# Moving 160 columns of the last down-projection chunk into an earlier load, and folding with two full-width products

## The chip, the core and the metric

The kernel runs on one core of a Trainium2 chip. Its time is the device time of one execution in microseconds (us). The median of three runs of the kernel before is 263.67 us (263.55 to 263.82).

## The reference

One decoding step of a transformer block for 8 sequences, in float32. Attention with 32 query heads over 4 key/value heads looks at the last 1024 cached positions; a gated feed-forward layer of width 3584 follows.

```python
h  = x + softmax(q(LN(x)) @ K.T * 128**-0.5) @ V @ wo      # K, V: last 1024 of 4096 positions
g  = LN(h) @ w_gate                                        # (8, 3584)
u  = LN(h) @ w_up
h2 = h + (gelu(g) * u) @ w_down                            # w_down: (3584, 1024)
```

The 111 MB of weights and caches are read once; the arithmetic on 8 rows is small.

## The kernel before

All weights and caches stream through two SBUF buffers, `wbuf[0]` and `wbuf[1]`, of 64 KB per partition each. One queue, SyncE's (SP), issues every load in program order: twelve units of 8 MB that alternate between the buffers, then the parts of `w_down`. `w_down` has 28 chunks of 128 rows. The first eight ride in other units. Sixteen go into `wbuf[0]` as `wd0` (12 chunks) and `wd1` (4). The last four go into `wbuf[1]`: `we0` holds two chunks (`last - 3` and `last - 2`), `we1` one (`last - 1`), and the last chunk, numbered `last`, is split by columns into `wl0` (160 of every 256 columns) and `wl1` (the other 96).

TensorE (PE) works with tiles of 128 x 32: four column groups of the array run side by side, each on its own 32 output partitions. Each product in float32 appears in the trace as two MATMUL records. In the tail, output partitions `32j .. 32j+31` hold columns `256j .. 256j+255` of the result, so that one chunk is four products of 256 columns (`QW`), one per column group.

A loop on PE (`half`, line 227 in the profile) makes the big products. Its last pass, `half_a(6)`, multiplies `wd0` and `wd1` and leaves the sums in the bank pair `sums[0]`. VectorE (DVE) adds these to the residual in the tile `d1` (lines 430 and 431). Behind the loop stands straight code on PE, in this order: chunks `last - 3` and `last - 2` into the bank `acc` (they wait for `we0`); the fold, four products of `add2` with `d1`, which bring `d1` into the layout by column groups; chunk `last - 1` (waits for `we1`); then the last chunk's 160 columns into the bank `fin` (wait for `wl0`) and its 96 columns into `sums[1]` (wait for `wl1`). ScalarE (ACT) copies the whole of `acc` to the tile `most` (line 450). DVE adds `most` and each bank into `o_fin` (line 464), and two stores of `o_fin` end the program: `out0` (160 columns) from SP's queue and `out1` (96 columns) from ACT's. Line 96 is the helper that issues every DMA. Three memsets on DVE, `ahead` (line 455), wait for `we1` ahead of the final adds. GpSimd (POOL) prepares constants at the start.

Of the kernel before, what the change touches and what calls it, by code (L numbers as in the profile page):

```python
# [7 lines left out]
P = 128  # L8
B = 8
D = 1024  # L10
# [5 lines left out]
NQ = 4  # L16
QW = D // NQ
N = 512
# [11 lines left out]
PARTS = (12, 4)  # L30
ENDPARTS = (2, 1)
ENDS = (160, 96)
# [12 lines left out]
class Flow:  # L45
# [37 lines left out]
    def run(self, engine, make, *waits, mark=True, gives=None):  # L83
        ins = self.start(engine, make, waits)
        if gives is not None:
            ins.then_inc(*gives)
            return None
        if not mark:
            return None
        self.done[engine] += 1  # L90
        ins.then_inc(self.own[engine], 1)
        return self.own[engine], self.done[engine]

    def move(self, name, out, src, *waits, engine="sync", sem=None):
        s = self.sem(name) if sem is None else sem
        self.start(engine, lambda e: e.dma_start(out, src), waits).then_inc(s, 16)  # L96
        return s, 16


def decode_block(nc, x, units, dn, tails, ends, outs):  # L100

    fl = Flow(nc)
    run, move = fl.run, fl.move
# [3 lines left out]
    def sb(name, *shape):  # L107
        return nc.alloc_sbuf_tensor(name, list(shape), F32).ap()

    def bank(name, n):  # L110
        return nc.alloc_psum_tensor(name, [P, n], F32).ap()

    space = sb("w", P, 2 * BUF)
    wbuf = [space[:, i * BUF:(i + 1) * BUF] for i in range(2)]
    sums = [bank(f"sum{i}", 2 * N) for i in range(2)]
    turned = bank("turned", 2 * N)
    acc, fin = bank("acc", N), bank("fin", N)
# [25 lines left out]
    def half_a(k, h=1):  # L143
        return at_mark["a", k, h]

    def half_b(k, h=1):
        return at_mark["b", k, h]
# [5 lines left out]
    for u in range(UNITS):  # L153
        k, i = divmod(u, 2)
# [7 lines left out]
    for i, (n, sem) in enumerate(zip(PARTS, (go[0], *go_later[1:]))):  # L162
        c0 = (q0 - EARLY) * D
# [2 lines left out]
    assert q0 == EARLY + HEAD  # L166
    arrived = {}
    c0 = 0
    for i, n in enumerate(ENDPARTS):
        here = move(f"we{i}", wbuf[1][:, c0:c0 + n * D], tails[i], half_b(nb - 1))  # L170
        for r in range(n):
            arrived[q0] = wbuf[1][:, c0 + r * D:c0 + (r + 1) * D], here
            q0 += 1
        c0 += n * D
    last = q0
    assert last == DF // P - 1
    blocks = []
    a = 0
    for i, (n, src) in enumerate(zip(ENDS, ends)):
        t = wbuf[1][:, c0:c0 + NQ * n]  # L180
        blocks.append((a, n, t, move(f"wl{i}", t, src)))
        c0 += NQ * n
        a += n


    ident = sb("ident", P, P)
    z = run("gpsimd", lambda e: e.memset(ident, 0.0))
# [8 lines left out]
    add2 = sb("add2", P, 2, 32)  # L196
    run("gpsimd", lambda e: e.tensor_add(
        add2.rearrange("p c m -> p (c m)"), ident[:, 0:2 * 32], ident[:, 2 * 32:4 * 32]), id_ok)
    note = sb("note", 1, 8)
    for i, g in enumerate(go_later):  # L200
        run("gpsimd", lambda e: e.memset(note[:, i:i + 1], 0.0), gives=(g, GATE[i] * (passes - 1)))

    own = sb("own", P, HB)
# [30 lines left out]
    with PE.Fori(1, TURNS) as i:  # L234
        with PE.If(i != NO_B[0]):
            with PE.If(i != NO_B[1]):
                half(1, [(0, (go[1], 17))])
                take(go_fold, 1)
                for ch in range(2):
                    ins = PE.matmul(turned[0:32, ch * N:(ch + 1) * N], add2[:, ch, :], y_sb,  # L240
                                    start=True, stop=True)
# [52 lines left out]
    for hf in range(2):  # L294
        done = (half_a, half_b)[hf]
        q_sb = sb(f"q{hf}", P, N)
        tok = run("vector", lambda e: e.tensor_scalar(  # L297
            q_sb, sums[hf][:, 0:N], scale, None, op0=ALU.mult), done(0, 0))
# [23 lines left out]
    for hf in range(2):  # L322
        done = (half_a, half_b)[hf]
        nmax, tot, rtot = (sb(f"{n}{hf}", P, 1) for n in ("nmax", "tot", "rtot"))
        share.append(sb(f"share{hf}", P, HB))
        tok = run("vector", lambda e: e.tensor_reduce(  # L326
            out=nmax, in_=sums[hf], axis=AX.X, op=ALU.max, negate=True), done(1))
# [5 lines left out]
        tok = run("vector", lambda e: e.reciprocal(rtot, tot), p_ok)  # L333
# [6 lines left out]
    for hf in range(2):  # L340
        done = (half_a, half_b)[hf]
        o_sb = sb(f"o{hf}", P, DH)
        tok = None
        for h in range(2):
            o3 = sums[hf][:, h * N:(h + 1) * N].rearrange("p (b d) -> p b d", b=HB)
            for b in range(HB):
                end = h == 1 and b == HB - 1
                out = source[:, hf * DH:(hf + 1) * DH] if end else o_sb
                if h == 0 and b == 0:
                    tok = run("vector", lambda e: e.tensor_scalar(  # L350
                        out, o3[:, b], share[hf][:, b:b + 1], None, op0=ALU.mult), done(2, h))
                else:
                    tok = run("vector", lambda e: e.scalar_tensor_tensor(  # L353
                        out, o3[:, b], share[hf][:, b:b + 1], o_sb, op0=ALU.mult, op1=ALU.add),
                        tok, done(2, h), mark=not end,
                        gives=(go_turn, 1) if end and hf else None)
# [11 lines left out]
    tok = run("scalar", lambda e: e.copy(y_sb, sums[0][:, 0:N]), half_a(3, 0))  # L368
    tok = run("vector", lambda e: e.tensor_add(y_sb, y_sb, sums[0][:, N:2 * N]), tok, half_a(3))  # L369
    tok = run("vector", lambda e: e.tensor_add(y_sb, y_sb, sums[1][:, 0:N]), tok, half_b(3, 0))  # L370
# [13 lines left out]
    at = sb("at", P, DF // P, 32)  # L384
# [3 lines left out]
    for k, n in enumerate(SETS):  # L388
        rows = 32 * n
        tok = run("scalar", lambda e: e.copy(gate[:rows], sums[0][:rows, 0:N]), half_a(4 + k, 0))  # L390
        tok = run("vector", lambda e: e.tensor_add(  # L391
            gate[:rows], gate[:rows], sums[0][:rows, N:2 * N]), tok, half_a(4 + k))
        ge_ok = run("scalar", lambda e: e.activation(ge[:rows], gate[:rows], AF.Gelu_apprx_tanh), tok)
        if k == 1:
# [5 lines left out]
        tok = run("scalar", lambda e: e.copy(up[:rows], sums[1][:rows, 0:N]), half_b(4 + k, 0))  # L400
        tok = run("vector", lambda e: e.tensor_add(  # L401
            up[:rows], up[:rows], sums[1][:rows, N:2 * N]), tok, half_b(4 + k))
        run("vector", lambda e: e.tensor_mul(source[:rows, 0:N], up[:rows], ge[:rows]), tok, ge_ok,
            gives=(go_turn, 1))
        t = turned[:, 0:N].rearrange("p (i m) -> p i m", m=P)
        at_ok = run("vector", lambda e: e.tensor_copy(
            at[:, q0:q0 + 4 * n, :].rearrange("p (j i) m -> p i j m", j=n),
            t[:, :, 0:rows].rearrange("p i (j m) -> p i j m", j=n)), at_mark["t", 6 + k])
# [6 lines left out]
        else:  # L415
# [3 lines left out]
                at_ok, gives=(go_later[0], 1))  # L419
# [3 lines left out]
    tok = run("vector", lambda e: e.tensor_add(  # L423
        down[rows:P], down[rows:P], sums[1][rows:P]), half_b(5), side_ok)
    for ch in range(2):
        p0 = 32 * (2 + ch)
        tok = run("vector", lambda e: e.tensor_copy(
            rest[p0:p0 + 32], down[rows:P, ch * N:(ch + 1) * N]), tok)
    d1 = sb("d1", P, N)
    tok = run("vector", lambda e: e.tensor_add(d1, rest, sums[0][:, 0:N]), tok, half_a(6, 0))  # L430
    d1_ok = run("vector", lambda e: e.tensor_add(d1, d1, sums[0][:, N:2 * N]), tok, half_a(6))


    def quarters(lhs, rhs, *waits, start=False, stop=False):
        for j in range(NQ):
            tok = run("tensor", lambda e: e.matmul(
                acc[32 * j:32 * j + 32, 0:QW], lhs(j), rhs(j), start=start, stop=stop),
                *waits, mark=(stop and j == NQ - 1))
        return tok

    def chunk(q, **flags):
        t, here = arrived[q]
        return quarters(lambda j: at[:, q, :], lambda j: t[:, j * QW:(j + 1) * QW], here, at_ok, **flags)

    chunk(last - 3, start=True)
    chunk(last - 2)
    quarters(lambda j: add2[:, j // 2, :], lambda j: d1[:, (j % 2) * QW:(j % 2) * QW + QW], d1_ok)
    tok = chunk(last - 1, stop=True)
    most = sb("most", P, QW)
    most_ok = run("scalar", lambda e: e.copy(most, acc[:, 0:QW]), tok)  # L450


    ahead = sb("ahead", 1, AHEAD)
    for i in range(AHEAD):
        run("vector", lambda e: e.memset(ahead[:, i:i + 1], 0.0), arrived[last - 1][1], d1_ok)

    o_fin = sb("o_fin", P, QW)
    done = []
    for (c0, n, t, here), d_ps in zip(blocks, (fin, sums[1])):
        for j in range(NQ):  # L460
            tok = run("tensor", lambda e: e.matmul(  # L461
                d_ps[32 * j:32 * j + 32, 0:n], at[:, last, :], t[:, j * n:(j + 1) * n],
                start=True, stop=True), here, d1_ok, mark=(j == NQ - 1))
        done.append(run("vector", lambda e: e.tensor_add(  # L464
            o_fin[:, c0:c0 + n], most[:, c0:c0 + n], d_ps[:, 0:n]), most_ok, tok))

    for e in both:
        nc.engines[e].br_ne(lap, 0, on_true="never", on_false="through")
    with nc.body("never", valid_engines=both):
        nc.regs_alu(lap, lap, 1, op=ALU.add)  # L470
        for e in both:
            nc.engines[e].br_lt(lap, 9, on_true="never", on_false="through").branch_hint(near[e])
    nc.switch_bb("through")

    cut = ENDS[0]
    sent = [move("out0", outs[0], o_fin[:, 0:cut], done[0]),
            move("out1", outs[1], o_fin[:, cut:QW], done[1], engine="scalar")]


    issued = fl.sem("issued")  # L480
# [86 lines left out]
```

## Time and profile before

| | |
|---|---|
| median of the runs | 263.67 us |
| profiled execution, its own time | 263.59 us |
| span of its profile | 262.3 us |
| TensorE busy, share of the span | 54% |
| VectorE busy | 17% |
| ScalarE busy | 5% |
| data moved, mean rate | 111.31 MB, 424 GB/s |

The profile's span runs from the first to the last instruction; the execution's time is 1.3 us longer. In a timeline the columns are the start in us from the span's beginning, the duration in us, the engine, the line, the operation with what it writes and reads, and in brackets the idle time ahead of it with what ended it. "PEld" is a load of weights into TensorE's array, which overlaps PE. The end of a MATMUL record is modelled, so its start is the safer number.

### The profile page before, as it was taken

To read this page: it belongs to the slowest core of one execution; us is meant where nothing else is said; L and a number is where in the kernel's file an instruction comes from. 1 tells how busy PE (TensorE), PEld (TensorE's weight loads), DVE (VectorE), ACT (ScalarE), POOL (GpSimd) and SP (SyncE) were. 2 spreads that over 40 slices of the span, in tenths; PEclk is the share of its full clock that TensorE was granted. 3 is DMA by queue.
4 is the path that set the end of the run, shared out by engine and by line. 5 is a ranking of instruction groups with operands and counts; after the bars stand their busy time and mean duration, and the time that the engine had idled before them with its cause. 6 is when DMAs were issued, how large, how long until landed. Compare 5 with 4: busy or idle time off the path is not lost. (4 is left out here: it accounts for less than half of the span.)

```text
span 262.3 us, 2262 instructions
## 1 busy us (share of the span) xinstructions
PE 141.3 (54%) x972; PEld 45.1 (17%) x972; DVE 43.8 (17%) x115; ACT 13.5 (5%) x19; POOL 7.7 (3%) x18
## 2 busy tenths in 40 slices
PE   0025805926606927707908508827709809409986
PEld 0021201212101312102302102122102202103232
DVE  0340200240100140400410100264100300100522
ACT  1000000000120010000000200000300000200000
POOL 5000100100000000100100000000000000000000
PEclk9999985986965995956966965975956956858999
DMA  8997997999799799979979998997999999799895
GB/s 320 485 470 330 480 480 340 460 480 460 340 480 480 320 480 480 460 340 480 480 320 480 480 420 380 480 480 320 480 480 400 400 480 480 320 440 480 370 424 226
DMA packets 2896, 111.31 MB, mean 424 GB/s; under 512 B 456, under 2 KB 712, under 8 KB 976
## 3 DMA queue, kind: packets, MB, share of 16 engines
q1 hardware_dynamic: 2736, 111.23, 98.4%
q10 hardware_dynamic: 160, 0.08, 0.1%
HBM read 111.18 MB, written 0.13 MB: 424 GB/s over the span
## 5 line engine op out<-in xcount | busy, mean ns | idle before, releaser
L227 PE MATMUL sum<-w,still 128*32 128x512 f32 x832 | 116.3, 721 | 96.8 <-PEq L214 96.8
L227 PEld LDWEIGHTS sum<-w,still 128*32 128x32 f32 x832 | 32.5, 130 | 176.8 <-issue 176.7
L245 PE MATMUL turned<-ident,source 128*128 128x128 f32 x64 | 10.4, 315 | 20.9 <-PEq L214 20.9
L245 PEld LDWEIGHTS turned<-ident,source 128*128 128x128 f32 x64 | 8.3, 161 | 26.2 <-issue 26.2
L240 PE MATMUL turned<-y_sb,add 128*32 128x512 f32 x24 | 11.3, 592 | 0.9 <-PEq L214 0.9
L326 DVE TENSOR_REDUCE nmax<-sum 128x1 f32<-128x1024 f32 x2 | 2.4, 1224 | 28.4 <-PE sum L227 28.4
L401 DVE TENSOR_TENSOR up<-up,sum 128x512 f32<-128x512 f32 (+1 forms) x2 | 1.4, 684 | 32.2 <-PE sum L227 32.2
L297 DVE TENSOR_SCALAR q<-sum 128x512 f32<-128x512 f32 x2 | 1.4, 692 | 25.7 <-PE sum L227 25.7
L282 DVE COPY still<-turned 128x1024 f32<-128x1024 f32 x4 | 4.7, 1219 | 4.2 <-PE turned L245 4.2
L391 DVE TENSOR_TENSOR gate<-gate,sum 128x512 f32<-128x512 f32 (+1 forms) x2 | 1.4, 686 | 23.8 <-PE sum L227 23.8
L353 DVE SCALAR_TENSOR_TENSOR o<-sum,share,o 128x128 f32<-128x128 f32 x12 | 4.2, 350 | 4.2 <-PE sum L227 3.8
L350 DVE TENSOR_SCALAR o<-sum,share 128x128 f32<-128x128 f32 x2 | 0.7, 350 | 22.9 <-PE sum L227 22.9
L328 ACT ACT_TABLE_LOAD x1 | 1.3, 1283 | 59.0 <-DVE nmax L326 59.0
L357 POOL MEMSET still<- 128x1024 f32 x2 | 1.9, 952 | 74.3 <-PE sum L227 74.3
L240 PEld LDWEIGHTS turned<-y_sb,add 128*32 128x32 f32 x24 | 2.6, 110 | 8.7 <-issue 8.7
L369 DVE TENSOR_TENSOR y_sb<-y_sb,sum 128x512 f32<-128x512 f32 x1 | 0.7, 689 | 16.0 <-PE sum L227 16.0
L370 DVE TENSOR_TENSOR y_sb<-y_sb,sum 128x512 f32<-128x512 f32 x1 | 0.7, 689 | 15.8 <-PE sum L227 15.8
L302 POOL MEMSET still<- 128x1024 f32 x2 | 1.9, 958 | 46.4 <-PE sum L227 46.4
L328 ACT ACTIVATE source<-sum,nmax 128x1024 f32<-128x1024 f32 x2 | 2.2, 1114 | 18.8 <-PE turned L245 18.8
L368 ACT COPY y_sb<-sum 128x512 f32<-128x512 f32 x1 | 0.6, 586 | 50.7 <-PE sum L227 50.7
L313 DVE COPY still<-turned 128x16 f32<-128x16 f32 x32 | 2.7, 161 | 2.1 <-PE turned L245 2.1
L390 ACT COPY gate<-sum 128x512 f32<-128x512 f32 (+1 forms) x2 | 1.2, 584 | 30.6 <-PE sum L227 30.6
(64 smaller groups left out, 43.3 us busy)
## 6 DMA issues: line engine op xcount, KB each, us to landing
w<-dn SPq DMA_DIRECT2D x1, 6144.0 KB, 24.1
w<-dn SPq DMA_DIRECT2D x1, 2048.0 KB, 28.7
w<-tails SPq DMA_DIRECT2D x1, 1024.0 KB, 13.3
w<-tails SPq DMA_DIRECT2D x1, 512.0 KB, 14.2
w<-ends SPq DMA_DIRECT2D x1, 320.0 KB, 14.6
w<-units SPq DMA_DIRECT2D x12, 29.5
w<-ends SPq DMA_DIRECT2D x1, 192.0 KB, 14.5
out<-o_fin SPq DMA_DIRECT2D x1, 80.0 KB, 1.6
```

Source lines behind the costliest of these rows:

```text
L227: ins = PE.matmul(sums[i][32 * j:32 * j + 32, h * N:(h + 1) * N], still[i][:, 32 * s:32 * s + 32], wbuf[i][:, s * N:(s + 1) * N], start=(c ...
L240: ins = PE.matmul(turned[0:32, ch * N:(ch + 1) * N], add2[:, ch, :], y_sb, start=True, stop=True)
L245: ins = PE.transpose(turned[:, n * P:(n + 1) * P], source[:, n * P:(n + 1) * P], ident)
L282: run("vector", lambda e: e.tensor_copy(still[i].rearrange("p (c j m) -> p c j m", c=NC, j=NQ), turned.rearrange("p (c m) -> p c m", c=NC) ...
L297: tok = run("vector", lambda e: e.tensor_scalar(q_sb, sums[hf][:, 0:N], scale, None, op0=ALU.mult), done(0, 0))
L302: cleared.append(run("gpsimd", lambda e: e.memset(still[hf], 0.0), done(0)))
L313: run("vector", lambda e: e.tensor_copy(to[:, :, b, s, a, REP * b:REP * b + REP].rearrange("p k (h i) -> p k h i", h=2), frm[:, s, a * HB ...
L326: tok = run("vector", lambda e: e.tensor_reduce(out=nmax, in_=sums[hf], axis=AX.X, op=ALU.max, negate=True), done(1))
L328: p_ok = run("scalar", lambda e: e.activation(source, sums[hf], AF.Exp, bias=nmax, accum_out=tot), tok, at_mark["t", 1 + hf])
L353: tok = run("vector", lambda e: e.scalar_tensor_tensor(out, o3[:, b], share[hf][:, b:b + 1], o_sb, op0=ALU.mult, op1=ALU.add), tok, done(2 ...
L357: cleared[hf] = run("gpsimd", lambda e: e.memset(still[hf], 0.0), done(2))
L391: tok = run("vector", lambda e: e.tensor_add(gate[:rows], gate[:rows], sums[0][:rows, N:2 * N]), tok, half_a(4 + k))
```

## The change

The load `we0` grows from two chunks to two chunks and the 160 columns of the last chunk; `wl0` is gone, and `wl` carries the 96 columns. The 160 columns are now accumulated into `acc`, together with chunks `last - 3` and `last - 2`. Chunk `last - 1` leaves `acc`: its first 160 columns go to `sums[1]`, its other 96 to `fin`, where the last chunk's 96 are added. ACT copies `acc` in two pieces straight into `o_fin`, and DVE adds the two banks to them in place. The second add into `d1` is cut into two halves of 256 columns, and the fold is now two products of 128 output columns with constants `fold` that POOL builds, placed ahead of the chunks. The two stores swap their queues.

```diff
+    cut = ENDS[0]
     for i, n in enumerate(ENDPARTS):
-        here = move(f"we{i}", wbuf[1][:, c0:c0 + n * D], tails[i], half_b(nb - 1))
+        size = n * D + (0 if i else NQ * cut)
+        here = move(f"we{i}", wbuf[1][:, c0:c0 + size], tails[i], half_b(nb - 1))
...
-    for i, (n, src) in enumerate(zip(ENDS, ends)):
-        t = wbuf[1][:, c0:c0 + NQ * n]
-        blocks.append((a, n, t, move(f"wl{i}", t, src)))
...
+    t = wbuf[1][:, c0:c0 + NQ * ENDS[1]]
+    rear = t, move("wl", t, ends)
...
+    fold = sb("fold", P, 2, P)
+    z = run("gpsimd", lambda e: e.memset(fold, 0.0))
+    for j in range(NQ):
+        run("gpsimd", lambda e: e.tensor_copy(fold[:, j % 2, 32 * j:32 * j + 32], add2[:, j // 2, :]), z)
...
-    d1_ok = run("vector", lambda e: e.tensor_add(d1, d1, sums[0][:, N:2 * N]), tok, half_a(6))
+    for i in range(2):
+        part = slice(i * QW, (i + 1) * QW)
+        d1_ok = run("vector", lambda e: e.tensor_add(
+            d1[:, part], d1[:, part], sums[0][:, N + i * QW:N + (i + 1) * QW]), tok, half_a(6))
+        run("tensor", lambda e: e.matmul(
+            acc[:, 0:QW], fold[:, i, :], d1[:, part], start=(i == 0), stop=False), d1_ok, mark=False)
...
-    chunk(last - 3, start=True)
-    chunk(last - 2)
-    quarters(lambda j: add2[:, j // 2, :], lambda j: d1[:, (j % 2) * QW:(j % 2) * QW + QW], d1_ok)
-    tok = chunk(last - 1, stop=True)
-    most = sb("most", P, QW)
-    most_ok = run("scalar", lambda e: e.copy(most, acc[:, 0:QW]), tok)
+    for q in (last - 3, last - 2):
+        quarters(acc, q, *arrived[q], 0, QW)
+    acc_ok = quarters(acc, last, *head, 0, cut, width=cut, stop=True)
+    ready = [quarters(sums[1], last - 1, *arrived[last - 1], 0, cut, start=True, stop=True)]
+    quarters(fin, last - 1, *arrived[last - 1], cut, QW, start=True)
+    ready.append(quarters(fin, last, *rear, 0, QW - cut, width=QW - cut, stop=True))
+    o_fin = sb("o_fin", P, QW)
+    pieces = ((0, cut), (cut, QW))
+    most = [run("scalar", lambda e: e.copy(o_fin[:, a:b], acc[:, a:b]), acc_ok) for a, b in pieces]
...
-    for (c0, n, t, here), d_ps in zip(blocks, (fin, sums[1])):
-        for j in range(NQ):
-            tok = run("tensor", lambda e: e.matmul(
-                d_ps[32 * j:32 * j + 32, 0:n], at[:, last, :], t[:, j * n:(j + 1) * n],
-                start=True, stop=True), here, d1_ok, mark=(j == NQ - 1))
-        done.append(run("vector", lambda e: e.tensor_add(
-            o_fin[:, c0:c0 + n], most[:, c0:c0 + n], d_ps[:, 0:n]), most_ok, tok))
+    done = [
+        run("vector", lambda e: e.tensor_add(o_fin[:, a:b], o_fin[:, a:b], d_ps[:, 0:b - a]), *toks)
+        for (a, b), d_ps, *toks in zip(pieces, (sums[1], fin), most, ready)
+    ]
...
-    sent = [move("out0", outs[0], o_fin[:, 0:cut], done[0]),
-            move("out1", outs[1], o_fin[:, cut:QW], done[1], engine="scalar")]
+    sent = [move("out0", outs[0], o_fin[:, 0:cut], done[0], engine="scalar"),
+            move("out1", outs[1], o_fin[:, cut:QW], done[1])]
```

On PE, the straight code behind the loop stands like this before (`add` is the constant tile `add2`; a row with x7 is seven more of the same):

```order
L436 MATMUL acc<-w,at 32x256 [waits we0_done,vector_done]
L436 MATMUL acc<-w,at 32x256 x7
L436 MATMUL acc<-d,add 32x256 [waits vector_done]
L436 MATMUL acc<-d,add 32x256 x3
L436 MATMUL acc<-w,at 32x256 [waits we1_done]
L436 MATMUL acc<-w,at 32x256 x3
L461 MATMUL fin<-w,at 32x160 [waits wl0_done]
L461 MATMUL fin<-w,at 32x160 x3
L461 MATMUL sum<-w,at 32x96 [waits wl1_done]
L461 MATMUL sum<-w,at 32x96 x3
```

And like this in the changed kernel (line 438 is the fold, line 444 the chunks):

```order
L438 MATMUL acc<-d,fold 128x256 [waits vector_done] x2
L444 MATMUL acc<-w,at 32x256 [waits we0_done]
L444 MATMUL acc<-w,at 32x256 x7
L444 MATMUL acc<-w,at 32x160 x4
L444 MATMUL sum<-w,at 32x160 [waits we1_done]
L444 MATMUL sum<-w,at 32x160 x3
L444 MATMUL fin<-w,at 32x96 x4
L444 MATMUL fin<-w,at 32x96 [waits wl_done]
L444 MATMUL fin<-w,at 32x96 x3
```

The fold has moved from behind the chunks of `we0` to the head, and became two products of 128 output columns in place of four of 32; behind `we1` now stand 160 and 96 columns of chunk `last - 1`, and behind the last load only four products of 96 columns.

On SP's queue, from the first part of `w_down` to the end, before (the two rows of `tails` are `we0` and `we1`, those of `ends` are `wl0` and `wl1`):

```order
L96 DMA w<-dn 128x12288 [waits tensor_done]
L96 DMA w<-dn 128x4096
L96 DMA w<-tails 128x2048 [waits tensor_done]
L96 DMA w<-tails 128x1024
L96 DMA w<-ends 128x640
L96 DMA w<-ends 128x384
L96 DMA out<-o_fin 128x160 [waits vector_done]
```

In the changed kernel:

```order
L96 DMA w<-dn 128x12288 [waits tensor_done]
L96 DMA w<-dn 128x4096
L96 DMA w<-tails 128x2688 [waits tensor_done]
L96 DMA w<-tails 128x1024
L96 DMA w<-ends 128x384
L96 DMA out<-o_fin 128x96 [waits vector_done]
```

The 640 elements per partition of `wl0` stand ahead of `we1` now, as a part of `we0`; one issue fewer is left, and the store from this queue is the one of 96 columns.

More of the change, by code (lines that the diff above doesn't have):

```diff
@@ L173, in decode_block @@
             q0 += 1
-        c0 += n * D
+        if i == 0:
+            head = wbuf[1][:, c0 + n * D:c0 + size], here
+        c0 += size
     last = q0
     assert last == DF // P - 1
-    blocks = []
-    a = 0
-    for i, (n, src) in enumerate(zip(ENDS, ends)):
-        t = wbuf[1][:, c0:c0 + NQ * n]
-        blocks.append((a, n, t, move(f"wl{i}", t, src)))
-        c0 += NQ * n
-        a += n
+    t = wbuf[1][:, c0:c0 + NQ * ENDS[1]]
+    rear = t, move("wl", t, ends)
     ident = sb("ident", P, P)
@@ L430, in decode_block, with quarters @@
     tok = run("vector", lambda e: e.tensor_add(d1, rest, sums[0][:, 0:N]), tok, half_a(6, 0))
-    d1_ok = run("vector", lambda e: e.tensor_add(d1, d1, sums[0][:, N:2 * N]), tok, half_a(6))
-    def quarters(lhs, rhs, *waits, start=False, stop=False):
+    for i in range(2):
[4 more added lines that the diff above has]
+            acc[:, 0:QW], fold[:, i, :], d1[:, part], start=(i == 0), stop=False), d1_ok, mark=False)
+    def quarters(d_ps, q, t, here, a, b, width=QW, start=False, stop=False):
         for j in range(NQ):
             tok = run("tensor", lambda e: e.matmul(
-                acc[32 * j:32 * j + 32, 0:QW], lhs(j), rhs(j), start=start, stop=stop),
-                *waits, mark=(stop and j == NQ - 1))
-        return tok
-    def chunk(q, **flags):
-        t, here = arrived[q]
-        return quarters(lambda j: at[:, q, :], lambda j: t[:, j * QW:(j + 1) * QW], here, at_ok, **flags)
-    chunk(last - 3, start=True)
-    chunk(last - 2)
-    quarters(lambda j: add2[:, j // 2, :], lambda j: d1[:, (j % 2) * QW:(j % 2) * QW + QW], d1_ok)
-    tok = chunk(last - 1, stop=True)
-    most = sb("most", P, QW)
-    most_ok = run("scalar", lambda e: e.copy(most, acc[:, 0:QW]), tok)
+                d_ps[32 * j:32 * j + 32, 0:b - a], at[:, q, :], t[:, j * width + a:j * width + b],
+                start=start, stop=stop), here, at_ok, mark=(stop and j == NQ - 1))
+        return tok
+    for q in (last - 3, last - 2):
[7 more added lines that the diff above has]
+    most = [run("scalar", lambda e: e.copy(o_fin[:, a:b], acc[:, a:b]), acc_ok) for a, b in pieces]
     ahead = sb("ahead", 1, AHEAD)
@@ L455, in decode_block @@
         run("vector", lambda e: e.memset(ahead[:, i:i + 1], 0.0), arrived[last - 1][1], d1_ok)
-    o_fin = sb("o_fin", P, QW)
-    done = []
-    for (c0, n, t, here), d_ps in zip(blocks, (fin, sums[1])):
-        for j in range(NQ):
-            tok = run("tensor", lambda e: e.matmul(
-                d_ps[32 * j:32 * j + 32, 0:n], at[:, last, :], t[:, j * n:(j + 1) * n],
-                start=True, stop=True), here, d1_ok, mark=(j == NQ - 1))
-        done.append(run("vector", lambda e: e.tensor_add(
-            o_fin[:, c0:c0 + n], most[:, c0:c0 + n], d_ps[:, 0:n]), most_ok, tok))
+    done = [
+        run("vector", lambda e: e.tensor_add(o_fin[:, a:b], o_fin[:, a:b], d_ps[:, 0:b - a]), *toks)
+        for (a, b), d_ps, *toks in zip(pieces, (sums[1], fin), most, ready)
+    ]
     for e in both:
@@ L473, in decode_block @@
     nc.switch_bb("through")
-    cut = ENDS[0]
-    sent = [move("out0", outs[0], o_fin[:, 0:cut], done[0]),
-            move("out1", outs[1], o_fin[:, cut:QW], done[1], engine="scalar")]
+    sent = [move("out0", outs[0], o_fin[:, 0:cut], done[0], engine="scalar"),
+            move("out1", outs[1], o_fin[:, cut:QW], done[1])]
     issued = fl.sem("issued")
@@ L532 @@
     at = [EARLY + HEAD + sum(ENDPARTS[:i]) for i in range(len(ENDPARTS))]
-    tails = np.concatenate([by_row(a, n) for a, n in zip(at, ENDPARTS)])
-    cuts = [sum(ENDS[:i]) for i in range(len(ENDS) + 1)]
+    tails = [by_row(a, n).reshape(P, -1) for a, n in zip(at, ENDPARTS)]
+    cut = ENDS[0]
     by_group = rows[-1].reshape(P, NQ, QW)
-    ends = np.concatenate([by_group[:, :, a:b].reshape(-1) for a, b in zip(cuts, cuts[1:])])
+    tails[0] = np.concatenate([tails[0], by_group[:, :, :cut].reshape(P, -1)], 1)
+    tails = np.concatenate([t.reshape(-1) for t in tails])
+    ends = by_group[:, :, cut:].reshape(P, -1)
     arrays = {
-        "x": own(A_x).reshape(B, D), "units": own(units), "dn": dn, "tails": tails, "ends": ends,
+        "x": own(A_x).reshape(B, D), "units": own(units), "dn": dn, "tails": tails, "ends": own(ends),
     }
@@ L549 @@
     outs = [o.rearrange("(p n) -> p n", p=P) for o in (out[0:cut], out[cut:P * QW])]
-    aps["ends"] = [
-        aps["ends"][P * NQ * a:P * NQ * b].rearrange("(p n) -> p n", p=P)
-        for a, b in zip(cuts, cuts[1:])
-    ]
-    for name, parts in (("dn", PARTS), ("tails", ENDPARTS)):
+    for name, parts, more in (("dn", PARTS, 0), ("tails", ENDPARTS, NQ * ENDS[0])):
         flat, f0 = aps[name], 0
         aps[name] = []
-        for n in parts:
-            aps[name].append(flat[f0:f0 + P * n * D].rearrange("(p n) -> p n", p=P))
-            f0 += P * n * D
+        for i, n in enumerate(parts):
+            size = P * (n * D + (0 if i else more))
+            aps[name].append(flat[f0:f0 + size].rearrange("(p n) -> p n", p=P))
+            f0 += size
     decode_block(nc, outs=outs, **aps)
```

## The prediction

> **What bounds the kernel now.** I read the page first. The DMA row is near full all along, so the loads set the pace, and the chain that ended last begins with a load of `ends`.
>
> ```profile
> DMA  8997997999799799979979998997999999799895
> GB/s 320 485 470 330 480 480 340 460 480 460 340 480 480 320 480 480 460 340 480 480 320 480 480 420 380 480 480 320 480 480 400 400 480 480 320 440 480 370 424 226
> DMA w<-ends 6%; PE sum L227 3%; SPq L96 0%; PE fin L461 0%; PE sum L461 0%; DVE o_fin L464 0%
> ```
>
> Then the chain in order of time: a load, eight records of 160 columns, eight of 96, one add, one store.
>
> ```profile
> 244.88 14.56 DMA w<-ends
> ...
> 259.49 0.48 PE fin L461 x8
> 259.96 0.40 PE sum L461 x8
> ...
> 260.39 0.26 DVE o_fin L464
> ```
>
> The timeline of the last stage shows what each engine does from the end of the loop on.
>
> ```profile
> 244.75 0.69 DVE L403 TENSOR_TENSOR source<-up,ge 96x512 f32<-96x512 f32 x1
> 245.59 1.09 PE L245 MATMUL turned<-ident,source 128*128 128x128 f32 x8
> 250.08 7.07 PE L227 MATMUL sum<-w,still 128*32 128x512 f32 x64 [1.56 <-PEq L214]
> 257.21 0.69 DVE L431 TENSOR_TENSOR d<-d,sum 128x512 f32<-128x512 f32 x1 [2.75 <-PE sum L227]
> 257.47 1.07 PE L436 MATMUL acc<-w,at 128*32 128x256 f32 x16 [0.32 <-DMA w<-tails]
> 258.33 0.64 PE L436 MATMUL acc<-d,add 128*32 128x256 f32 x8
> 258.67 0.26 PEld L436 LDWEIGHTS acc<-w,at 128*32 128x32 f32 x8 [0.17 <-DMA w<-tails]
> 258.76 0.64 PE L436 MATMUL acc<-w,at 128*32 128x256 f32 x8
> 259.46 0.37 ACT L450 COPY most<-acc 128x256 f32<-128x256 f32 x1 [18.28 <-PE acc L436]
> 259.49 0.48 PE L461 MATMUL fin<-w,at 128*32 128x160 f32 x8
> 259.95 0.16 PEld L461 LDWEIGHTS sum<-w,at 128*32 128x32 f32 x8 [0.31 <-DMA w<-ends]
> 259.95 0.37 PE L461 MATMUL sum<-w,at 128*32 128x96 f32 x8
> 260.03 0.32 DVE L464 TENSOR_TENSOR o_fin<-most,fin 128x160 f32<-128x160 f32 x1 [1.17 <-PE fin L461]
> 260.39 0.26 DVE L464 TENSOR_TENSOR o_fin<-most,sum 128x96 f32<-128x96 f32 x1
> 260.68 0.35 ACTq L96 DMA_DIRECT2D out<-o_fin  x1
> ```
>
> PE is out of the loop at 257.15 and then waits for each load in turn: `we0` until 257.4, `we1` until 258.7, `wl0` until 259.5, `wl1` until 259.95. Between these waits it has time to spare. So before the change the tail is bound by the arrival of data, and the last four products start as soon as `wl1` is there. The store issued at 260.68 ends the span.
>
> **Rates read from these rows.** Four products of 256 columns take 0.43 us (starts at 258.33 and 258.76; two chunks from 257.47 to 258.33), so 160 columns take 0.27 and 96 take 0.16. From the end of that streaming to the start of the engine that waits for it pass 0.27 us (258.76 + 0.43 to ACT at 259.46; 259.49 + 0.27 to DVE at 260.03). The clock was full there:
>
> ```profile
> 256.00:258.00 2.00, 1.68 (x24) 0.59 (x20) 0.69 (x1) 0.00 (x0) 0.00 (x0) 1.00 0.98 392
> 258.00:260.00 2.00, 1.92 (x40) 0.85 (x36) 0.12 (x3) 0.37 (x1) 0.00 (x0) 1.00 0.58 219
> ```
>
> (the columns ahead of the last two are busy times by engine, then the granted clock: 1.00 in both). Durations by width, from the groups of instructions (mean ns stands behind the bar):
>
> ```profile
> L431 DVE TENSOR_TENSOR d<-d,sum 128x512 f32<-128x512 f32 x1 | 0.7, 689 | 2.7 <-PE sum L227 2.7
> L464 DVE TENSOR_TENSOR o_fin<-most,fin 128x160 f32<-128x160 f32 x1 | 0.3, 320 | 1.2 <-PE fin L461 1.2
> L464 DVE TENSOR_TENSOR o_fin<-most,sum 128x96 f32<-128x96 f32 x1 | 0.3, 255 | 0.0
> L400 ACT COPY up<-sum 96x512 f32<-96x512 f32 x1 | 0.6, 582 | 12.4 <-PE sum L227 12.4
> L450 ACT COPY most<-acc 128x256 f32<-128x256 f32 x1 | 0.4, 373 | 18.3 <-PE acc L436 18.3
> L313 DVE COPY still<-turned 128x16 f32<-128x16 f32 x32 | 2.7, 161 | 2.1 <-PE turned L245 2.1
> ```
>
> An add of 256 columns on DVE lies on the line through 160 and 512: 320 + 96 x 369/352 = 0.42 us. ACT's copies of 160 and 96 lie on the line through 256 and 512 (0.82 ns a column): 0.29 and 0.24. Independent DVE instructions overlap: 32 copies of 161 ns took 2.7 us, 84 ns apart, so a second half starts up to 0.08 before the first one's end.
>
> **The loads.** Bytes and order of the stream stay, apart from 320 KB that move ahead of `we1`.
>
> ```profile
> w<-tails SPq DMA_DIRECT2D x1, 1024.0 KB, 13.3
> w<-tails SPq DMA_DIRECT2D x1, 512.0 KB, 14.2
> w<-ends SPq DMA_DIRECT2D x1, 320.0 KB, 14.6
> w<-ends SPq DMA_DIRECT2D x1, 192.0 KB, 14.5
> ```
>
> By the ends of PE's waits (257.42, 258.67, 259.48, 259.95) the last three come 1.25 us (512 KB), 0.81 (320 KB) and 0.47 (192 KB) apart: 0.0024 to 0.0025 us per KB for rows of 4096, 2560 and 1536 bytes alike, so I price the longer row and the missing load at nothing. PE sees the new arrivals at 257.42 + 0.81 = 258.2 (`we0`), 259.5 (`we1`) and 259.95 (`wl`, as `wl1` now). One issue of 0.43 us less on SP is worth nothing either: the loads wait 13 to 15 us in the queue behind it. That queue is the cover.
>
> **The fold.** It is the costly part. Before, four products on four column groups ran side by side in 0.43 us, at a time when PE had `we1` still to wait for (0.17 us). Now two products fill all 128 columns and run one after the other, 256 columns each. A product alone takes as long as four side by side, so I take 2 x 0.43 = 0.86. The trace has no full-width product in two records; the transposes of line 245 are the nearest (eight starts in 0.83 us for 128 columns, one record each; two records of 256 columns at that rate are 4 x 0.12 = 0.48, so 0.43 is no overestimate). The low end is 0.21 a product, if one record did it.
>
> The fold now stands first and waits for DVE. Its first half is done at 257.21 + 0.42 = 257.63. From DVE to PE I take 0.09: between the 0.15 from line 403 (end 245.44) to the transposes (245.59), which pass through a wait of their own, and the 0.03 from DVE to the issue of a store (260.65 to 260.68). The fold starts at 257.72. The second half is ready between 257.98 and 258.06, plus 0.09, just when the first product ends (258.15): no stall. PE is through with the fold at 258.58.
>
> **From full width back to tiles of 32 columns.** At one place the trace shows this switch, behind the transposes:
>
> ```profile
> 246.20 0.49 PE L245 MATMUL turned<-ident,source 128*128 128x128 f32 x3
> ...
> 246.62 0.14 PEld L249 LDWEIGHTS fin<-idle 128*32 128x32 f32 x2 [0.17 <-issue]
> 246.62 0.62 PE L249 MATMUL fin<-idle 128*32 128x512 f32 x1
> ```
>
> The last transpose started at 246.42 (its record lasts 0.27), the array was free 0.11 later, and the next product started at 246.62: 0.09 lost, with a branch in between that may be part of it. I take 0.10; the bounds are 0 and 0.38 (emptying the array, 0.27, and then loading weights, 0.11). The Trainium skill, "TensorEngine Tiling (Array Packing)", Tiling Modes, Key Properties, says that changing the tiling mode drains the engine; it speaks against this change and gives no price. The trace agrees that there is a gap; by the page's rule with the full 0.27 seen here the sum would be 0.17 higher. The first switch, ahead of the fold, falls into 0.57 us in which PE idles anyway.
>
> **The rest of the chain, now on PE.** 258.68: chunks `last - 3` and `last - 2`, 0.86, to 259.54 (`we0` is there at 258.2). The 160 columns, 0.27, to 259.81. Chunk `last - 1`, 0.27 and 0.16 (`we1` at 259.5), to 260.24. The last 96 columns, 0.16 (`wl` at 259.95), to 260.40. PE never waits for a load, with 0.3 to 0.5 us to spare at each; it needs 257.72 to 260.40 for work that used to end at 260.11, and became the bound.
>
> ACT starts at 259.81 + 0.27 = 260.08; its copies end at 260.37 and 260.61. DVE's first add starts at 260.42 (0.04 from ACT, an estimate by the 0.03 from DVE to the store) and ends at 260.74. The second needs `fin` (260.40 + 0.27 = 260.67), ACT (260.65) and DVE itself (260.66 to 260.74): start 260.72, end 260.98. The three are within 0.1 us of each other, so shortening one alone brings little. The store is issued at 261.01 instead of 260.68: **+0.33 us**. It takes as long as before; its queue is SP's instead of ACT's, and both issues took 0.35. Behind it SP still has only the clearing of semaphores to do while the data lands. The first store sits on ACT's queue with nothing behind it.
>
> The `ahead` memsets wait for `we1`, now 0.8 later (259.5); they take 0.12 and the adds behind them start at 260.42, so they are covered. POOL's memset and four copies fall between 4.3 and about 6 us:
>
> ```profile
> 3.97 0.32 POOL L197 TENSOR_TENSOR add<-ident 128x64 f32<-128x64 f32 x1
> 4.23 0.12 POOL L201 MEMSET note<- 1x1 f32 x2
> 10.33 1.27 DVE L260 BATCH_NORM_STATS2 ln_bn<-x_sb 32x6 f32<-32x512 f32 x2 [7.83 <-DMA x_sb<-x]
> ```
>
> DVE waits for `x` until 10.33, and the notes behind POOL's new work open loop gates that are needed only in the last passes. Cost: nothing.
>
> **Sum.** The profiled execution took 263.59 us, 0.08 below the median of 263.67. Its 263.59 + 0.33 is 263.92; on the median, 264.00. With all bounds on the short side (0.03 from DVE, no switch, full overlap on DVE) the store moves by 0.15; with 0.15 from DVE, a switch of 0.27 and no overlap, by 0.56. A shift of 0.2%, 0.53 us, is about what a measurement of this kernel can tell from no change, so +0.33 counts as within it.
>
> **Rivals.**
> - *The tail stays bound by the last load.* If a full-width product costs 0.21, the fold ends at 258.32 (its second half of `d1` is there only at 258.11), and PE is ready for the last four products at 259.98, as `wl` is there at 259.95: the end moves by 0.03 to 0.06, 263.7. For it: transposes go in one record each. Against: every other float32 product in the trace is two records. Chance 0.15.
> - *The switch empties the array*: slower by over 0.2%. Place: between fold and chunks, at 258.58. Price 0.38 instead of 0.10, so +0.61, 264.28. It decides from 0.30 on. For it: the gap behind the transposes exists, and no weights were loaded ahead across it (the load started with the product, at 246.62). Against: that gap was 0.09 in all. Chance 0.17.
> - *The stream ends earlier.* Rows of 10752 bytes in place of 8192 could move at the 480 GB/s of the page's best slices, not the 420 of these loads: 1344 KB would then take 0.4 us less, and the time, if PE followed, would be 263.2. PE can't follow by these rows: even with the cheap fold it is ready at 259.98, so something that frees it sooner would have to join. Against it also: three row lengths, one rate. Chance 0.04, with all that the trace doesn't show on this side.
>
> **How the numbers follow.** The forecast, PE as the bound with +0.15 to +0.53, has the remaining 0.64; its own range is 263.8 to 264.2. The range over all, 263.5 to 264.35, takes in the first two rivals and the 0.15 by which single runs differ from the median. Slower by over 0.2%: the second rival and a remnant of the forecast, 0.18. Faster by over 0.2%: 0.04. Within: 0.78.
>
> **What would show it.** PE's idle time for `tails` and `ends` is gone from the tail; the fold's four records start near 257.7 and the chunks near 258.7; the last products start at 260.2 although `wl` was there at 259.95; the chain that ended last runs from line 227 over DVE, fold and chunks, not from a load. A chain that still begins with `ends` shows the first rival, a first chunk product at 258.9 or later the second. I would be wrong if landing times moved by more than those 0.3 to 0.5 us, or if some engine stalled on something that this trace doesn't show.

## The result, and the profile after

The changed kernel takes 264.17 us (median of 16 runs, 264.02 to 264.46) against 263.69 us before (median of 16). The ratio is 1.0017 with a 95% interval of 1.0009 to 1.0025: a loss of 0.48 us by the medians (0.45 by the ratio), clear of zero and below the 0.2% that the prediction set as its limit. The profiled execution took 264.02 us, its span is 262.7 us.

The chain that ended last, in order of time (start, length, what), no longer holds a load:

```profile
250.03 7.11 PE sum L230 x64
...
257.17 0.43 DVE d L436
257.60 0.04 issue
257.64 1.13 PE acc L438 x4
258.77 1.32 PE acc L444 x24
...
260.11 0.30 ACT o_fin L457
...
260.51 0.10 DVE o_fin L465
...
260.86 0.13 DVE o_fin L465
```

Before, it ran from a load of `ends` straight into the last products. Now it starts in the loop (line 230 is the old 227) and passes DVE's half add, the fold (line 438), the chunks (line 444), ScalarE's copy and the two adds. The granted clock was 1.00 from 250 to 260 us in both profiles, so the clock has no part in what differs there. The timeline of the tail:

```profile
257.17 0.75 DVE L436 TENSOR_TENSOR d<-d,sum 128x256 f32<-128x256 f32 x2 [2.75 <-PE sum L230]
257.64 1.13 PE L438 MATMUL acc<-d,fold 128*128 128x256 f32 x4 [0.53 <-DVE d L436]
258.70 1.34 PE L444 MATMUL acc<-w,at 128*32 128x256 f32 x24
259.86 0.45 PE L444 MATMUL sum<-w,at 128*32 128x160 f32 x8
260.11 0.43 ACT L457 COPY o_fin<-acc 128x160 f32<-128x160 f32 x2 [18.18 <-PE acc L444]
260.13 0.51 PE L444 MATMUL fin<-w,at 128*32 128x96 f32 x16
260.51 0.32 DVE L465 TENSOR_TENSOR o_fin<-o_fin,sum 128x160 f32<-128x160 f32 x1 [0.95 <-ACT o_fin L457]
260.75 0.25 DVE L465 TENSOR_TENSOR o_fin<-o_fin,fin 128x96 f32<-128x96 f32 x1
260.86 0.35 ACTq L96 DMA_DIRECT2D out<-o_fin  x1
261.02 0.35 SPq L96 DMA_DIRECT2D out<-o_fin  x1
```

No PE row from 258.70 on has a wait in brackets. The loads were there in time; first their issues on SP in the timeline, then the list of issues, where the last number is the time from issue to landing:

```profile
244.78 0.80 SPq L96 DMA_DIRECT2D w<-tails  x2
245.63 0.43 SPq L96 DMA_DIRECT2D w<-ends  x1
```

```profile
w<-tails SPq DMA_DIRECT2D x1, 1344.0 KB, 13.2
w<-tails SPq DMA_DIRECT2D x1, 512.0 KB, 14.2
w<-ends SPq DMA_DIRECT2D x1, 192.0 KB, 14.2
```

`we0` was issued at 244.78 and landed near 258.0, 0.7 ahead of the first chunk product; `wl`, issued at 245.63, landed near 259.8, 0.5 ahead of the last products, which start near 260.3.

### The profile page after: what moved, and what is told of

Read it like the earlier page. It is cut to its first block, busy times and chain, and to the rows that moved or that the text cites. A ratio compares the mean times of both kernels' runs of the same rounds, so it can differ in the third digit from the quotient of the medians.

```text
span 262.7 us, 2276 instructions
## 1 busy us (share of the span) xinstructions
PE 143.2 (54%) x976; PEld 46.0 (18%) x976; DVE 43.8 (17%) x116; ACT 13.6 (5%) x20; POOL 8.6 (3%) x23
## 5 line engine op out<-in xcount | busy, mean ns | idle before, releaser
L230 PE MATMUL sum<-w,still 128*32 128x512 f32 x832 | 117.9, 730 | 95.1 <-PEq L217 95.1
```

Of the source, the lines that this page charges most:

```text
L230: ins = PE.matmul(sums[i][32 * j:32 * j + 32, h * N:(h + 1) * N], still[i][:, 32 * s:32 * s + 32], wbuf[i][:, s * N:(s + 1) * N], start=(c ...
```

## The experiments

All are read in two ways: by the median, and in the profile by the distance from the start of the add into `d1` behind the loop to the issue of the last store. The second leaves out that the loop ends a few tenths of a microsecond earlier or later from one execution to the next. That distance is 3.47 us before (257.21 to 260.68) and 3.85 in the changed kernel (257.17 to 261.02).

**The narrow fold in the wide one's place** (changed kernel; POOL's constants are left out too).

```diff
-        run("tensor", lambda e: e.matmul(
-            acc[:, 0:QW], fold[:, i, :], d1[:, part], start=(i == 0), stop=False), d1_ok, mark=False)
+        for j in (i, i + 2):
+            run("tensor", lambda e: e.matmul(
+                acc[32 * j:32 * j + 32, 0:QW], add2[:, j // 2, :], d1[:, part], start=True, stop=False),
+                d1_ok, mark=False)
```

> The changed kernel with the fold as four products on the four column groups, at the same place: two behind each half of d1. POOL's constants for it are left out. Theory (TensorE's own work is the bound of the tail): the fold's last streaming ends at about 258.05 + 0.43 = 258.48 instead of 258.61, and the gap of 0.09 behind it goes, so the first chunk product starts near 258.5 instead of 258.70, the last four products near 260.08 instead of 260.29, and the last store is issued near 260.8 instead of 261.02: 0.2 us less than the changed kernel, about 263.95. Rival A (the tail waits for loads): chunks and last products start when they did, no change. Rival B (the later `we0` is what costs): no change either, and the chunks start at a load's arrival.

Measured: 263.80 us (11 runs), ratio to the kernel before 1.0000 (0.9991 to 1.0009).

```profile
257.42 0.75 DVE L432 TENSOR_TENSOR d<-d,sum 128x256 f32<-128x256 f32 x2 [2.75 <-PE sum L226]
257.89 0.74 PE L435 MATMUL acc<-d,add 128*32 128x256 f32 x6 [0.53 <-DVE d L432]
258.35 0.41 PE L442 MATMUL acc<-w,at 128*32 128x256 f32 x2
258.46 0.39 PE L435 MATMUL acc<-d,add 128*32 128x256 f32 x2
...
260.95 0.35 SPq L96 DMA_DIRECT2D out<-o_fin  x1
```

From the add to the last store 3.53 us, 0.32 less than in the changed kernel; the median fell by 0.37, where 0.2 was expected. The first chunk product even starts at 258.35, ahead of the fold's last records at 258.46: the second records of the fold's first half start at 258.13 and are 0.21 long, so two of the four column groups were free by then. Everything else of the change stayed in. So 0.37 of the 0.48 us go with the width of the fold, and what is left can't be told from the kernel before. The chain that ended last holds no load here either, but little room is left: `we1` (issued at 245.10, 14.5 us to landing) landed at 259.62, and the first product that reads it starts at 259.67.

**The wide fold alone** (kernel before, with d1 in halves and the two wide products at the head).

```diff
-    d1_ok = run("vector", lambda e: e.tensor_add(d1, d1, sums[0][:, N:2 * N]), tok, half_a(6))
+    for i in range(2):
+        part = slice(i * QW, (i + 1) * QW)
+        d1_ok = run("vector", lambda e: e.tensor_add(
+            d1[:, part], d1[:, part], sums[0][:, N + i * QW:N + (i + 1) * QW]), tok, half_a(6))
+        run("tensor", lambda e: e.matmul(
+            acc[:, 0:QW], fold[:, i, :], d1[:, part], start=(i == 0), stop=False), d1_ok, mark=False)
...
-    chunk(last - 3, start=True)
+    chunk(last - 3)
     chunk(last - 2)
-    quarters(lambda j: add2[:, j // 2, :], lambda j: d1[:, (j % 2) * QW:(j % 2) * QW + QW], d1_ok)
```

> The kernel before with one part of the change alone: d1 in two halves, and the fold in two full-width products at the head; loads, banks, copy and stores as before. Theory: the chunks start at 258.70 (behind fold and gap), chunk `last - 1` at 259.56, the 160 columns at 259.99, the 96 at 260.26; ScalarE's one copy of 256 columns runs from 260.26 to 260.63; the adds start near 260.67 and 260.91; the last store at 261.2, 0.5 us later than before: 264.2. Rival A (a tail bound by loads): the last store stays at 260.68, 263.7.

Measured: 264.39 us, ratio 1.0025 (1.0016 to 1.0034).

```profile
257.18 0.75 DVE L437 TENSOR_TENSOR d<-d,sum 128x256 f32<-128x256 f32 x2 [2.75 <-PE sum L231]
257.65 1.13 PE L439 MATMUL acc<-d,fold 128*128 128x256 f32 x4 [0.54 <-DVE d L437]
258.72 1.50 PE L445 MATMUL acc<-w,at 128*32 128x256 f32 x24
...
260.29 0.37 ACT L458 COPY most<-acc 128x256 f32<-128x256 f32 x1 [18.29 <-PE acc L445]
...
260.76 0.32 DVE L472 TENSOR_TENSOR o_fin<-most,fin 128x160 f32<-128x160 f32 x1 [1.94 <-PE sum L469]
261.00 0.25 DVE L472 TENSOR_TENSOR o_fin<-most,sum 128x96 f32<-128x96 f32 x1
...
261.28 0.35 ACTq L96 DMA_DIRECT2D out<-o_fin  x1
```

The store is 0.60 later than before (0.5 was expected), the median 0.70: by the medians this part alone costs more than the whole change (0.48). The 95% intervals of the two ratios overlap, but the distance from the add to the last store says the same, 4.10 against 3.85. The rest of the change seems to give something back on top of a wide fold: here `acc` is closed only behind chunk `last - 1`, and ScalarE copies it from 260.29 in one piece, where the changed kernel starts at 260.11 and hands over the first piece after 0.30.

**The loads alone** (changed kernel with the fold of the kernel before, behind the chunks of `we0`, and d1 in one piece; POOL's constants are left out too).

```diff
-    for i in range(2):
-        part = slice(i * QW, (i + 1) * QW)
...
+    d1_ok = run("vector", lambda e: e.tensor_add(d1, d1, sums[0][:, N:2 * N]), tok, half_a(6))
...
-        quarters(acc, q, *arrived[q], 0, QW)
+        quarters(acc, q, *arrived[q], 0, QW, start=(q == last - 3))
+    for j in range(NQ):
+        run("tensor", lambda e: e.matmul(
+            acc[32 * j:32 * j + 32, 0:QW], add2[:, j // 2, :], d1[:, (j % 2) * QW:(j % 2) * QW + QW],
+            start=False, stop=False), d1_ok, mark=False)
```

> The changed kernel with the fold of the kernel before: d1 added in one piece, four narrow products behind the two chunks of `we0`; merged load, banks, copies and stores as changed. Theory: the chunks start when `we0` is there (near 258.05), the fold at 258.9, the 160 columns at 259.33, chunk `last - 1` at 259.6, the last four products at 260.03; the last store near 260.75, 0.1 later than before: 263.75 to 263.85. Rival B (the merged load costs by its later arrival): chunks start at 258.2 or later and the last store at 260.95 or later.

Measured: 264.02 us, ratio 1.0012 (1.0003 to 1.0021): a loss of 0.33, where 0.08 to 0.18 was expected. The chain that ended last and the timeline:

```profile
245.15 12.89 DMA w<-tails
258.05 0.14 issue
258.18 1.07 PE acc L435 x16
```

```profile
258.18 1.07 PE L435 MATMUL acc<-w,at 128*32 128x256 f32 x16 [1.07 <-DMA w<-tails]
259.04 0.64 PE L443 MATMUL acc<-d,add 128*32 128x256 f32 x8
259.47 0.48 PE L435 MATMUL acc<-w,at 128*32 128x160 f32 x8
...
260.92 0.35 SPq L96 DMA_DIRECT2D out<-o_fin  x1
```

The bigger load lands at 258.05 as assumed, but the first product starts 0.13 behind the landing; PE stands idle for 1.07 us in front of it. From there on it is bound by its own work: the last store is issued 0.24 later than before. This comes within 0.03 of rival B (258.2 and 260.95): with the old fold, the merged load costs by its later arrival. In the changed kernel the fold fills that hole, and is longer than the hole.

**The stores' queues put back** (changed kernel).

```diff
-    sent = [move("out0", outs[0], o_fin[:, 0:cut], done[0], engine="scalar"),
-            move("out1", outs[1], o_fin[:, cut:QW], done[1])]
+    sent = [move("out0", outs[0], o_fin[:, 0:cut], done[0]),
+            move("out1", outs[1], o_fin[:, cut:QW], done[1], engine="scalar")]
```

> The changed kernel with the queues of the two stores as before: 160 columns from SP, 96 from ACT. The store's issue should stay at 261.0. Theory C (the changed queues cost the 0.08 us by which the span grew more than the last store's issue): from the last issue to the end of the span 1.58 as before instead of 1.65, 264.1. Rival D (the two stores are now issued 0.16 us apart instead of 0.30, so their data meet): 1.65 stays.

Measured: 264.14 us, 0.03 below the changed kernel.

```profile
261.02 0.35 SPq L96 DMA_DIRECT2D out<-o_fin  x1
261.19 0.35 ACTq L96 DMA_DIRECT2D out<-o_fin  x1
```

From the last issue to the end of the span (262.84) pass 1.66 us here, 1.67 in the changed kernel, 1.58 before. So the queues are not the reason (theory C falls, up to 0.01 us); the wide fold alone, whose stores have the queues of the kernel before, has 1.64 as well. All seven experiments have their stores 0.15 to 0.17 apart, and all lie between 1.64 and 1.68; the kernel before has them 0.30 apart. That fits rival D, but no kernel here changes that distance alone. Nor do the packets of the last store take longer: in the traces they pass in 0.32 us before and after. What grew is the time from the issue to their start (0.87 before, 0.93 in the changed kernel) and from their end to the landing (0.36 and 0.40).

**Later loads** (changed kernel, one more load of 128 KB ahead of `we0`).

```diff
+    spare = sb("spare", P, 256)
+    spare_in = move("spare", spare, tails[1][:, 0:256], half_b(nb - 1))
```

> The changed kernel with one more load of 128 KB ahead of `we0` on the same queue, into a tile that nothing reads: by the 0.0024 us per KB of the tail, `we0`, `we1` and `wl` come about 0.31 us later each. Theory (TensorE's work is the bound, with 0.3 to 0.5 us to spare at each load): chunks and last products start as in the changed kernel, 264.15 to 264.25. Rival A (the tail is bound by loads): the last store moves by the whole 0.31, 264.48.

Measured: 264.15 us (11 runs), the changed kernel's 264.17 within noise. In the profiled execution the loop ended 0.65 later, so the distances count:

```profile
246.43 0.91 SPq L96 DMA_DIRECT2D w<-tails  x2
...
257.82 0.75 DVE L438 TENSOR_TENSOR d<-d,sum 128x256 f32<-128x256 f32 x2 [2.75 <-PE sum L232]
...
259.36 1.34 PE L446 MATMUL acc<-w,at 128*32 128x256 f32 x24
...
261.67 0.35 SPq L96 DMA_DIRECT2D out<-o_fin  x1
```

```profile
w<-tails SPq DMA_DIRECT2D x1, 1344.0 KB, 12.6
```

From the add to the last store 3.85, as in the changed kernel, although `we0` (issued at 246.43, 12.6 us to landing) came 1.2 behind the start of the add, against 0.8 in the changed kernel: 0.4 later, where 0.31 was expected. `we1` and `wl` come 0.4 later too. The chunks still start 1.06 behind the fold, as in the changed kernel, and the products of `we1` and `wl` still start 0.15 behind the landing of their loads, instead of 0.5. So the loads have room in the changed kernel, and the tail is not bound by them; a delay of 0.4 uses up most of it.

**One more pair of width changes** (changed kernel; the extra product's result isn't used).

```diff
+        if i == 0:
+            run("tensor", lambda e: e.matmul(
+                turned[0:32, 0:64], idle[:, 0:32], idle[:, 0:64], start=True, stop=True), mark=False)
```

> The changed kernel with a small product between the two of the fold: 32 output columns, 64 columns long, of zeros, into a bank that nobody reads. It adds two changes of tile width, and 0.11 us of streaming. Theory (a change costs about 0.10, as behind the transposes and behind the fold): the chunks start 0.3 to 0.4 later than in the changed kernel, 264.45 to 264.6. Rival E (the array is emptied and loaded anew at each change, 0.38): 0.87 later, 265.0. Rival F (the gap is no price of the change of width): 0.11 later, 264.3.

Measured: 264.69 us (5 runs), 0.52 more than the changed kernel and a little above the 264.45 to 264.6 expected.

```profile
257.41 0.75 DVE L436 TENSOR_TENSOR d<-d,sum 128x256 f32<-128x256 f32 x2 [2.75 <-PE sum L230]
257.88 0.70 PE L438 MATMUL acc<-d,fold 128*128 128x256 f32 x2 [0.53 <-DVE d L436]
258.51 0.30 PE L441 MATMUL turned<-idle 128*32 128x64 f32 x2
258.74 0.70 PE L438 MATMUL acc<-d,fold 128*128 128x256 f32 x2
259.37 1.34 PE L447 MATMUL acc<-w,at 128*32 128x256 f32 x24
```

From the fold's first start to the chunks 1.49 instead of 1.06: 0.43 more, 0.11 of it the small product's streaming. That leaves 0.32 for two changes of width, 0.16 each with what comes with them. The small product starts 0.63 behind the pair's first record: 0.32 to the second record, 0.21 for its streaming, 0.10 of gap. The gap behind the small product, back to full width, is 0.10 too (its second record starts at 258.59 and streams for 0.05; the next starts at 258.74). Most of the rest is the start of the second full-width stream, whose first two records stand 0.32 apart again (258.74 and 259.06) instead of 0.21. Rivals E (0.87) and F (0.11) fall.

**d1 in one piece, wide fold** (changed kernel).

```diff
-        d1_ok = run("vector", lambda e: e.tensor_add(
-            d1[:, part], d1[:, part], sums[0][:, N + i * QW:N + (i + 1) * QW]), tok, half_a(6))
+    d1_ok = run("vector", lambda e: e.tensor_add(d1, d1, sums[0][:, N:2 * N]), tok, half_a(6))
```

> The changed kernel with the second add into d1 in one piece; both full-width products wait for it. Theory (the chain of the tail starts on VectorE): the fold starts at 257.21 + 0.69 + 0.04 = 257.94 instead of 257.64, everything behind it 0.3 later, 264.45. Rival A (loads): no change.

Measured: 264.48 us (8 runs), 0.31 more than the changed kernel.

```profile
257.36 0.69 DVE L434 TENSOR_TENSOR d<-d,sum 128x512 f32<-128x512 f32 x1 [2.74 <-PE sum L230]
258.10 1.13 PE L437 MATMUL acc<-d,fold 128*128 128x256 f32 x4 [0.80 <-DVE d L434]
...
261.48 0.35 SPq L96 DMA_DIRECT2D out<-o_fin  x1
```

The fold starts 0.27 later behind the loop, and the last store too (4.12 instead of 3.85). Every tenth that the fold starts later ends up in the time, so the chain does begin on DVE.

## Why the prediction was right, and where it was off

- **What bounds the tail.** Right: PE's own work took the place of the arrival of the loads. The chain of the profile after, the narrow fold (0.37 less), the later loads (nothing) and the whole d1 (0.31 more) show it from four sides. The size was too small: 0.33 us was predicted, 0.48 measured, which leaves 264.17 near the upper end of the forecast's 263.8 to 264.2.
- **Start of the fold.** 257.72 was predicted, 257.64 measured. Half of this is no merit or fault of the prediction: in this execution the loop ended earlier, and the add starts at 257.17 instead of 257.21. The rest is the step from DVE to PE, 0.04 (257.60 to 257.64) instead of the 0.09 that was put between 0.03 and 0.15.
- **Length of the fold.** 0.86 was predicted, 0.97 measured: four records at 257.64, 257.96, 258.18 and 258.39, the last 0.21 long. The spacing is the predicted 0.21 except behind the first record, where it is 0.32. The prediction had no term for this start of the stream:

```profile
257.64 0.48 PE L438 MATMUL acc<-d,fold 128*128 128x256 f32 x1 [0.53 <-DVE d L436]
257.64 0.30 PEld L438 LDWEIGHTS acc<-d,fold 128*128 128x128 f32 x2 [1.44 <-DVE d L436]
```

The first record starts together with the load of its own weights and is 0.10 longer than the other three (0.48 against 0.38). The two loads shown, each 0.19 long, are over at 257.94, so the second record, at 257.96, does not wait for its weights. By these rows it is the first load, about 0.11 of it, that nothing hides.

- **Back to narrow tiles.** 0.10 predicted; 258.39 + 0.21 to 258.70 is 0.10. By the Trainium skill, "TensorEngine Tiling (Array Packing)", Tiling Modes, Key Properties, a change of tiling mode drains the engine. The runs agree that a change of width costs time: 0.10 here, 0.10 at each of the two changes that the run with one more pair adds, and nothing visible where the width stays the same (with the narrow fold a chunk product starts at 258.35, right at 258.13 + 0.21). They show too that it is less than the 0.27 from the end of streaming to a waiting engine. What these 0.10 consist of, they don't show.
- **Chunks to copy.** 258.68 and 260.08 predicted for the first chunk and ScalarE's start; 258.70 and 260.11 measured. Counted from the start of the add, as the experiments are, both come 0.06 to 0.07 later than predicted.
- **The final adds.** 260.42 and 260.72 predicted, 260.51 and 260.75 measured. The first add waits for two semaphores and starts 0.10 behind the copy, not 0.04; the overlap of the two adds is the predicted 0.08 (260.83 to 260.75).
- **The last store.** 261.01 predicted, 261.02 measured. That they agree so closely is partly luck, as the loop ended 0.04 earlier in this execution: from the add to the store, 3.80 was predicted and 3.85 measured.
- **Behind the store.** Here is the largest part of what the sum lacks: "It takes as long as before" put 0 on the path behind the last issue, and 0.09 was measured (1.67 against 1.58). The changed queues were not it; the smaller distance of the two stores, 0.16 in place of 0.30, is a cause that fits but was not isolated. With it, 0.34 + 0.09 = 0.43, the difference of the two profiled executions (264.02 and 263.59). By the distance from the add, which leaves out where the loop ended, it is 0.38 + 0.09 = 0.47, and the medians differ by 0.48, against 0.33 predicted.
- **The rivals.** The tail bound by the last load falls with the narrow fold and the later loads. The emptied array would have cost 0.28 more than the forecast; it costs nothing beyond the 0.10 taken. The stream did not end much sooner: `wl` landed near 259.8, about 0.1 ahead of where `wl1` was before, and PE was not ready for it.
- **An open point.** The narrow fold with all the rest of the change equals the kernel before within its interval, by distance 0.06 longer. No run came out ahead of the kernel before. A likely reason is that its PE waits for each load anyway and that the four products behind the last one are short; no run tests it.

## What to carry to other kernels

When a tail waits for loads, add up the work that the waiting engine does in those waits before lengthening any of it: here a fold of 0.43 us fitted, one of 0.97 did not. Two full-width float32 products were no substitute here for four narrow ones that run side by side on the column groups: half as many instructions, more than twice the time, and a gap at the change of width. And moving bytes ahead in a load stream delays what the next engine needs first: the merged load, with its banks and copies but the old fold, cost 0.33 us, although no byte was added. With the narrow fold ahead of the chunks, in the time in which PE waits for that load, the same loads cost nothing that can be told from noise.

## What was not expected of the hardware

- The first two records of a stream of full-width float32 products stand 0.32 us apart, the others 0.21, with the first record 0.10 longer. It shows each time the stream starts anew (twice in the run with one more pair of width changes). At the start of the chunks, with tiles of 32 columns, it is 0.24: in the changed kernel the first four records start from 258.70 to 258.72, the next four from 258.94 to 258.96. The weight load of a full-width record takes 0.19, that of a transpose of the same width 0.14 and that of a 32-column tile 0.11.
- A product on a free column group doesn't wait for the end of the earlier ones on other groups: with the narrow fold a chunk product on a free group starts at 258.35, while the fold's last records on the other groups start at 258.46.
- The last store took 1.64 to 1.68 us from issue to the end of the span whenever another store had been issued 0.15 to 0.17 ahead of it, 1.58 with 0.30 between them.
